# Cosine attention and a Fourier-mixing feed-forward block on one core: new planner costs and step priorities for a list-scheduled kernel

## The chip, the cores and the metric

The kernel runs on one core of a Trainium2 chip. The core has TensorE (matrix multiply, PE in the profile), VectorE (DVE), ScalarE (ACT), GpSimd (POOL) and SyncE (SP), each with its own queue of instructions that it runs in order. Here POOL and SP also issue the DMA transfers. Engines wait for each other through semaphores. The metric is the time on the device, in microseconds (us).

## The reference

```python
q, k, v: (8, 12, 448, 64) float32; w_ch1: (768, 3072); w_ch2: (3072, 768)
q_n = q / (norm(q, axis=-1) + 1e-06);  k_n likewise
attn = softmax(q_n @ k_n.T / tau)                    # per batch and head
x = (attn @ v).transpose(0, 2, 1, 3).reshape(B, S, H * D)      # (8, 448, 768)
mixed = real(fft(fft(x, axis=1), axis=2))
u = x + mixed
un = (u - mean(u)) / sqrt(var(u) + 1e-06)
out = u + relu(un @ w_ch1) @ w_ch2                   # (8, 448, 768) float32
```

## The kernel before

Python code records some 2,900 steps of all 8 batches (`Plan.add`), each with the engines that may run it, an estimated duration, a priority, and what it reads and writes. `Plan.schedule` then places them on a time axis with a list scheduler, and `Plan.emit` writes one queue for each engine in the order that came out, with semaphore waits where a step needs another engine's result. So the order on every engine, and the choice between VectorE, ScalarE and POOL for some steps, follow from the estimated durations (`t_act`, `t_dve` and numbers at each step), the latencies `SEM_LAT` and `PE_LAT`, the modelled DMA flow (`FLOW`), and the priorities, to which the table `SHIFT` adds a number for single steps. Nothing of this runs on the chip; a step that comes later there than the planner thought holds up what stands behind it in its queue.

Step names end in the batch. For each batch b:

- `ld_k`, `ld_q`, `ld_t` load q and k (`t` is the last 64 rows of both). Batches 0 and 1 (`first_norm`) load two groups of six heads; each group g has `ld_k<g>`, `ld_q<g>` and `ld_t<g>` on SP (L661). Batch 1's are written into the place of the second weight matrix (`W2b`) before that is loaded. Later batches (`norm`) load rows into three buffers STG (L788).
- `sq` (ScalarE, L668 and L797) squares, `ss` (VectorE, L670 and L799) sums by head, `ln`, `nrm`, `eps`, `rcp` make the reciprocal norm, `sc` scales (L699 on VectorE or POOL, L806 on POOL). `tk`, `tq`, `tt` transpose on TensorE in batches 0 and 1 (L723, L735, L748); `tr` are DMA transposes into QT and KT from batch 2 on (L812).
- `qk` is a score step on TensorE (L880, L892), `ex` the exponential on ScalarE (L858), `pv` the product with v (L911, L917), `rd` and `x` the division on VectorE.
- `fa`, `f`, `g` fold the rows for the Fourier transform, `fs` (L1004) and `fd` (L1042) are its two matrix products, `u` adds x (L1070, tiles of U), `bs`, `ba`, `ln2`, `rs`, `un` are the layer norm (L1099 to L1108), `tn` (TensorE, L1118, with evictions L1126) or `tru` (DMA, L1129) transposes it into UNT.
- `h` is the first FFN layer (L1176), `relu` its eviction (L1192), `y` and `m` are the second layer (L1207), `fin`, `fa..p` add the residual U on VectorE and POOL (L1239, L1232), `st` and `sc_` store. From batch 1 on the second layer of two tiles at once is done with seven products in place of eight; `s` and `t` are the sums for that.

Attention of batch b + 1 is interleaved with the FFN of batch b on TensorE. `Plan.fill` puts groups of six filler matmuls (`warm`, L1418) into gaps that the planner expects on TensorE. The weights are loaded by POOL in 24 chunks (L592, L593); the first W1 chunk's landing opens batch 1's loads.

The planner's rule for a step that needs results:

```python
else:
    t = max(t, d.end + (SEM_LAT if d.eng != "pe" else PE_LAT) + ...)
...
op.start = t
free[e] = t + d
op.end = t + d
```

Of the kernel before, what the change touches and what calls it, by code (L numbers as in the profile page):

```python
# [24 lines left out]
SEM_LAT = 0.11  # L25
PE_LAT = 0.2
DMA_LAT = 2.0
FLOW = {r"W1_\d+": (3.66, 2.3, 1.25), r"W2_\d+": (3.48, 1.95, 2.6), r"ld_v\d_[01]": (4.35, 1.2, 0.35), r"ld_v\d_\d": (2.92, 1.81, 1.2),
        r"ld_t\d_[01]": (2.95, 1.3, 0.8), r"ld_[kq]\d_[01]": (2.34, 1.92, 0.86), r"ld_t\d_\d": (2.8, 1.75, 1.2), r"ld_[kq]\d_\d": (2.07, 1.65, 0.85),
# [3 lines left out]
    "iota": {0: -840.7}, "cst": {0: -19.8}, "tqd": {0: -145.4}, "tps": {0: -28.6, 1: -75}, "vz0": {0: 9.3}, "vz1": {0: 285.2}, "ldt0": {0:  # L33
# [44 lines left out]
}  # L78

LATE = {r"W[12]_\d+": 1.5, "tmd": 2.0, r"sq\d_2": 4.0, r"sq\d_\d": 2.0, r"ktd\d": 3.0, r"qdup\d": 3.0, r"qk\d._[2-7]": 1.5, r"pv\d\d_[2-7]": 2.0, r"pv\d\d_1": 1.0, r"h\d+_[1-7]": 0.3}
PIECE = {r"sc[KQ]\d_0": 0.95, r"scT\d_0": 0.42, r"sc\d_\d": 0.6, r"f[avm]\dp_\d": 0.54, r"t\d\d": 0.94}
PORT = r"eps\d|f[a01]\d_\d|g\d_\d|u\d+_\d|un\d_\d|s\d\d_\d|t\d\d|sc[KQT]\d_\d"

# [1391 lines left out]
```

## Time and profile before

| | |
|---|---|
| runs | 590.57 us median of 3 (589.21 to 591.01) |
| span of the profiled execution | 590.7 us |
| the profiled execution's own time | the same 590.7 us: the profile has no other |
| busy | PE 571.0, DVE 417.8, ACT 355.0, POOL 211.1 us |
| first FFN matmul (L1176) | 53.67 us |
| last matmul ends | about 587.0 us |
| mean granted clock of TensorE | 0.993 |

Busy time of TensorE counts fillers and work at a lower clock like any other. Where its line in the 40 slices shows a digit under 9, it waited; where it shows 9, the order of its rows says whether the work was real. A wait on another engine matters only where it ends in a wait, a filler or a lower clock of TensorE.

### The profile page before, as it was taken

Reading aid. Unit: us, or ns where it says so; the run is one execution under the profiler, and the core shown is the slowest. Engines: PE = TensorE matmul, PEld = TensorE weight load, DVE = VectorE, ACT = ScalarE, POOL = GpSimd, SP = SyncE. Lnnn points to the kernel's source line nnn. Section 1 sums busy time; section 2 is a strip of 40 time slices with the busy share of each in tenths; the row PEclk is TensorE's granted clock in tenths of the full one; section 3 lists DMA queues with packets and bytes.
Section 4 is the critical chain, followed back from the end, with each engine's and each line's share of the span. In section 5 each row is a group of like instructions: output and inputs, shape, how many; then the busy total and the mean of one; then the engine's idle time right before and its main releaser. Section 6 shows DMA issues by size and latency. Waiting matters only on the chain.

```text
span 590.7 us, 15088 instructions
## 1 busy us (share of the span) xinstructions
PE 571.0 (97%) x6178; PEld 445.1 (75%) x6178; DVE 417.8 (71%) x970; ACT 355.0 (60%) x684; POOL 211.1 (36%) x316
## 2 busy tenths in 40 slices
PE   4897999999999999999999999999999999999997
PEld 3677888687787786878778688778788688778684
DVE  8887878997587767897788678867858547922222
ACT  7994896356874487568746767358566663224140
POOL 7733424346344623703281436440551210200302
PEclk9997999999999999999999999999999999999999
DMA  8999999684396854965496239483294110120101
GB/s 194 184 220 166 162 164 154 152 157 96 106 118 91 144 87 96 171 114 101 50 155 125 52 111 129 108 130 73 54 151 58 28 56 1 62 61 14 47 9 54
DMA packets 187637, 62.12 MB, mean 105 GB/s; under 512 B 166704, under 2 KB 185392, under 8 KB 187568
## 3 DMA queue, kind: packets, MB, share of 16 engines
q1 hardware_dynamic: 129648, 38.35, 33.4%
q0 software_dynamic: 57920, 22.81, 30.7%
q8 instruction: 48, 0.79, 0.6%
q14 instruction: 21, 0.17, 0.1%
HBM read 51.90 MB, written 11.01 MB: 107 GB/s over the span
## 4 chain that ended last, share of the span: by engine, by line
PE 88%; DMA 5%; POOL 2%; issue 1%; SPq 1%; DVE 1%; ACT 0%; POOLq 0%; DVEq 0%
PE PS L1176 37%; PE PS L1207 33%; PE PS L917 5%; PE PS L880 5%; DMA W2b<-in_q_dram 3%; PE PS L1004 2%; PE PS L911 2%; PE PS L1042 2%; DMA W1b<-in_moe_w_ch_dram 1%; SPq L661 1%; DMA KT<-QH 1%; PE PS L892 1%; PE PS L893 1%; POOL VB L838 1%; PE PS L1418 0%
## 5 line engine op out<-in xcount | busy, mean ns | idle before, releaser
L1176 PE MATMUL PS<-UNT,W1b 128*128 128x256 bf16 (+1 forms) x2304 | 237.3, 260 | 0.4 <-DMA UNT<-F 0.4
L1176 PEld LDWEIGHTS PS<-UNT,W1b 128*128 128x128 bf16 x2304 | 199.9, 98 | 23.3 <-issue 3.5
L858 ACT ACTIVATE E<-PS 128x900 bf16<-128x900 f32 (+1 forms) x192 | 148.0, 829 | 28.6 <-PE PS L880 25.0
L1207 PE MATMUL PS<-W2b,HQ 128*128 128x384 bf16 x768 | 133.8, 326 | 0.0
L1192 ACT ACTIVATE HQ<-PS 128x512 bf16<-128x512 f32 x122 | 72.8, 597 | 91.0 <-PE PS L1176 89.6
L806 POOL TENSOR_TENSOR QH<-STG,SM 128x256 bf16<-128x256 f32 x126 | 80.5, 664 | 95.4 <-DVE SM L615 81.9
L1207 PEld LDWEIGHTS PS<-W2b,HQ 128*128 128x128 bf16 x768 | 73.8, 98 | 46.0 <-issue 1.7
L1302 DVE TENSOR_TENSOR HQ<-HQ 128x512 bf16<-128x512 bf16 x141 | 62.6, 463 | 43.8 <-ACT HQ L1192 26.7
L1232 POOL TENSOR_TENSOR OUTB<-OUTB,U 128x192 f32<-128x192 f32 x66 | 39.0, 611 | 140.5 <-ACT OUTB L1227 140.2
L1207 PE MATMUL PS<-TX,HQ 128*128 128x384 bf16 x396 | 70.4, 326 | 0.0
L1207 PEld LDWEIGHTS PS<-TX,HQ 128*128 128x128 bf16 x396 | 37.9, 98 | 23.9 <-issue 0.4
L917 PE MATMUL PS<-VB,E 128*128 128x65 bf16 x1152 | 50.9, 193 | 0.0
L797 ACT ACTIVATE QH<-STG 128x384 f32<-128x384 f32 x84 | 42.3, 519 | 10.2 <-DVE SM L799 8.5
L917 PEld LDWEIGHTS PS<-VB,E 128*128 128x128 bf16 x1152 | 47.5, 97 | 1.1 <-ACT E L858 0.2
L799 DVE TENSOR_REDUCE SM<-QH 128x6 f32<-128x384 f32 x84 | 44.3, 543 | 5.1 <-ACT QH L797 4.6
L1192 DVE TENSOR_SCALAR HQ<-PS 128x512 bf16<-128x512 f32 x40 | 27.6, 691 | 25.9 <-PE PS L1176 25.5
L1261 POOL DMA_INDIRECT out_dram<-OUTB,IDX x20 | 20.6, 1029 | 70.6 <-DVE OUTB L1239 49.4
L911 PE MATMUL PS<-VZ,E 128*128 128x130 bf16 x192 | 41.6, 219 | 0.5 <-DMA VZ<-in_v_dram 0.5
L880 PE MATMUL PS<-QT,KT 64*128 64x225 bf16 x576 | 39.6, 259 | 1.2 <-DMA KT<-QH 0.4
L1070 DVE TENSOR_TENSOR U<-ACG,X 128x384 bf16<-128x384 f32 (+3 forms) x70 | 39.1, 580 | 0.8
L1239 DVE TENSOR_TENSOR OUTB<-PS,OUTB 128x384 f32<-128x384 f32 x33 | 18.2, 553 | 26.6 <-PE PS L1207 24.8
L1227 ACT ACTIVATE OUTB<-PS 128x384 f32<-128x384 f32 x33 | 16.2, 492 | 34.5 <-PE PS L1207 34.3
(133 smaller groups left out, 637.8 us busy)
## 6 DMA issues: line engine op xcount, KB each, us to landing
STG<-in_k_dram SPq DMA_DIRECT2D x18, 384.0 KB, 4.1
STG<-in_q_dram SPq DMA_DIRECT2D x18, 384.0 KB, 3.8
VB<-in_v_dram POOLq DMA_DIRECT2D x24, 192.0 KB, 5.3
W1b<-in_moe_w_ch_dram POOLq DMA_DIRECT2D x12, 384.0 KB, 8.8
W2b<-in_moe_w_ch_dram POOLq DMA_DIRECT2D x12, 384.0 KB, 6.4
out_dram<-OUTB SPq DMA_DIRECT2D x7, 384.0 KB
TX<-in_k_dram SPq DMA_DIRECT2D x2, 576.0 KB, 5.2
TX<-in_q_dram SPq DMA_DIRECT2D x2, 576.0 KB, 6.4
```

Of the source, the lines that this page charges most:

```text
L797: P.add("act", lambda a, sq=sq, src=buf[:, w * x:w * x + w]: a.activation(sq, src, ACTF.Square), t_act(w), pr, f"sq{i}_{b}", reads=bn, wri ...
L799: P.add("dve", lambda v, o=SS[:, i, H // ns * x:H // ns * (x + 1)], sq=sq: v.tensor_reduce(o, sq.rearrange("p (h d) -> p h d", d=DH), AX.X ...
L806: r = v.tensor_tensor(v3(qh)[:, h:h + 4], v3(buf)[:, h:h + 4], RN[:, i, h:h + 4].unsqueeze(2).to_broadcast((128, 4, DH)), AluOp.mult)
L858: return a.activation(o, self.PS[:, bk:bk + nc_, 0:SQ2], ACTF.Exp, scale=1.0 / self.tau)
L880: i = pe.matmul(self.PS[:, bk + h, c0:c0 + NK], self.KT[r, jj, kt * 128:(kt + 1) * 128], self.QT[r, jj, cols], start=True, stop=True)
L911: r = pe.matmul(o, st(6), self.VZ[:, j, :], start=not split, stop=(split and i == 0), skip_group_check=True)
L917: r = pe.matmul(o[:, 65 * h:65 * h + 65], st(2 * kt + h), self.VB[:, kt, 2 * j + h, :], start=(split and i == h == kt == 0), stop=((not sp ...
L1070: return v.tensor_tensor(U[o0:o0 + n, ut, cs].rearrange("p (i e) -> p i e", e=2), src, X[i0:i0 + n, x, cs].rearrange("p (i e) -> p i e", e ...
L1176: r = pe.matmul(self.PS[:, bk, x * n:(x + 1) * n], self.W1b[:, j, ft * 128:(ft + 1) * 128], self.UNT[:, j, cs], start=(j == 0), stop=(j == ...
L1192: return e.activation(o, i, ACTF.Relu) if e is self.nc.scalar else e.tensor_relu(o, i)
L1207: r = pe.matmul(self.PS[:, bk, 0:n], lhs(f), rhs(f), start=(start and f == 0), stop=(stop and f == NF // 2 - 1), skip_group_check=True)
L1302: P.add("dve", lambda v: v.tensor_tensor(cs(o), cs(a), cs(bq), op), 0.46, -0.5, f"{nm}{k}_{b}", reads=rd, writes=hr(o)(k))
```

## The change

1. The two latencies become a pipeline delay for each producer's engine (`PIPE`: the time from the end of an engine's hold to the result) and a hop for each waiting engine (`HOP`). An engine is free after its hold, and the result is there `PIPE` later.
2. The durations are replaced by holds: new formulas, and a table `OCC` by step name.
3. TensorE's step that follows a score step is charged `EXIT`.
4. The planner lets SP issue a load when the fourth DMA before it is nearly done, not the second.
5. `SHIFT` is another table.
6. U's tiles 3 and 6, which hold the last rows of two batches, are written and read under the names of their two halves in every batch, also where a batch uses them as whole tiles. This adds order between batches.

No step is added or taken away, except fillers: 40 groups before, 22 after. Lines of the file move by 14 to 18 (L661 to L679, L668 to L686, L699 to L717, L880 to L898, L1176 to L1194, L1207 to L1225, L1418 to L1435).

```diff
-SEM_LAT = 0.11
-PE_LAT = 0.2
+HOP = {"act": 0.035, "dve": 0.035, "pe": 0.058, "pool": 0.08, "sp": 0.1}
+PIPE = {"act": 0.108, "dve": 0.083, "pe": 0.165, "pool": 0.06, "sp": 0.0}
+EXIT = 0.065
+OCC = {"act": {r"ln\d": 0.195, r"ln2\d_\d": 0.185, ...}, "dve": {...}, "pe": {...}, "pool": {...}}
...
 SHIFT = {
-    "iota": {0: -840.7}, "cst": {0: -19.8}, "tqd": {0: -145.4}, ...
...
+    "ss4_7": {0: -620.6}, "rcp7": {6: -153.2}, "pv00_7": {0: 48.1}, ...
...
-        self.durs = durs
+        self.durs = tuple(next((x for n, x in OCC.get(e, {}).items() if re.fullmatch(n, name)), d) for e, d in zip(engs, durs))
...
-        flow, now, sync = {"sp": [], "pool": []}, 0.0, [None, None]
+        flow, now, sync = {"sp": [], "pool": []}, 0.0, [None] * 4
...
-                    t = max(t, d.end + (SEM_LAT if d.eng != "pe" else PE_LAT) + (...))
+                    t = max(t, d.end + HOP[e] + (...))
...
-                        rt = max(rt, sync[-2].end - DMA_LAT if sync[-2] else 0.0)
+                        rt = max(rt, sync[-4].end - DMA_LAT if sync[-4] else 0.0)
...
+            if e == "pe":
+                if split and op.name[:2] != "qk":
+                    t += EXIT
+                split = op.name[:2] == "qk"
...
-            op.end = t + d
+            op.end = t + d + (PIPE[e] if op.dma is None else 0.0)
...
-    return 0.12 + 0.00089 * n + 0.093 * ptr
+    return 0.061 + 0.000836 * n + 0.093 * ptr
...
-    return 0.1 + n / (960.0 * mode)
+    return 0.067 + n / (960.0 * mode)
...
-                    uadd(A0, 0, 0, 0, 128, hi, 0, f"U{A0}")
+                    uadd(A0, 0, 0, 0, 128, hi, 0, [f"U{A0}z0", f"U{A0}z64"] if A0 in (3, 6) else [f"U{A0}"])
...
-    def unames(self, b, ut):
-        Zt = self.utiles(b)[3]
-        return [f"U{ut}l", f"U{ut}h"] if ut != Zt else [f"U{ut}z{z}{x}" for z in (0, 64) for x in "lh"]
+    def unames(self, ut):
+        return [f"U{ut}l", f"U{ut}h"] if ut not in (3, 6) else [f"U{ut}z{z}{x}" for z in (0, 64) for x in "lh"]
```

More of the change, by code (lines that the diff above doesn't have):

```diff
@@ L190, in schedule @@
         port = []
-        free = {"pe": 1.0, "act": 2.0, "dve": 1.0, "pool": 0.85, "sp": 0.7}
-        flow, now, sync = {"sp": [], "pool": []}, 0.0, [None, None]
+        free = {"pe": 1.0, "act": 2.0, "dve": 1.0, "pool": 0.25, "sp": 0.7}
+        flow, now, sync = {"sp": [], "pool": []}, 0.0, [None] * 4
         def rtime(op, e):
@@ L199, in rtime @@
                 else:
-                    t = max(t, d.end + (SEM_LAT if d.eng != "pe" else PE_LAT) + (op.late if d.dma is not None or d.eng == "pool" and op.late >= 1 else op.margin if e == "pe" else 0.0))
+                    t = max(t, d.end + HOP[e] + (op.late if d.dma is not None or d.eng == "pool" and op.late >= 1 else op.margin if e == "pe" else 0.0))
             return t
@@ L231, in schedule @@
                 put(op)
-        left = len(self.ops)
+        left, split = len(self.ops), False
         slots = {n: [None] * k for n, k in self.pools.items()}
@@ L241, in slot_time @@
                 elif all(u.end is not None for u in t.users):
-                    free_at.append((max(u.end for u in t.users) + SEM_LAT, i))
+                    free_at.append((max(u.end for u in t.users) + 0.04, i))
             n = len(op.acquire)
@@ L340, in fill @@
                     new.deps.add(after)
-                    new.deps.add([o for o in self.order["dve"] if o.end + PE_LAT <= at + 0.1][-1])
+                    new.deps.add([o for o in self.order["dve"] if o.end <= at][-1])
                     new.deps.update(u for a, b, tile in live[bank[0]] if b <= t for u in tile.users[-2:] if u.eng != "pe")
@@ L667, in first_norm @@
                 sq = sqb[g][i]
-                sqo = P.add("act", lambda a, sq=sq, buf=buf: a.activation(sq, buf, ACTF.Square), t_act(64 * n), pg[g], f"sq{nm}{g}_{b}",
+                sqo = P.add("act", lambda a, sq=sq, buf=buf: a.activation(sq, buf, ACTF.Square), t_act(64 * n) + 0.034, pg[g], f"sq{nm}{g}_{b}",
                       reads=names, writes=sqn[g][i], order=[self.exps[-1]] if b else [])
@@ L702, in fn @@
                                                .to_broadcast((128, 3, 2, DH)), AluOp.mult)
-                    sc.append(P.add("dve" if b else ("dve", "pool"), fn, ((t_dve(21 * n), 0.95) if i < 2 else (0.3, 0.42)) if b == 0 else t_dve(21 * n) if i < 2 else 0.3, pg[g] + 0.1 * j, f"sc{nm}{jj}_{b}", reads=names + [f"RN_{g}{i}"],
+                    sc.append(P.add("dve" if b else ("dve", "pool"), fn, ((t_dve(21 * n), 0.95) if i < 2 else (0.2, 0.42)) if b == 0 else t_dve(21 * n) if i < 2 else 0.2, pg[g] + 0.1 * j, f"sc{nm}{jj}_{b}", reads=names + [f"RN_{g}{i}"],
                                     writes=qhn[g][i] if j == 0 else [qhn[g][i][-1] + f"_{j}"],
@@ L797, in norm @@
                 P.add("act", lambda a, sq=sq, src=buf[:, w * x:w * x + w]: a.activation(sq, src, ACTF.Square),
-                      t_act(w), pr, f"sq{i}_{b}", reads=bn, writes=sqn)
+                      t_act(w) + 0.034, pr, f"sq{i}_{b}", reads=bn, writes=sqn)
                 P.add("dve", lambda v, o=SS[:, i, H // ns * x:H // ns * (x + 1)], sq=sq: v.tensor_reduce(
@@ L858, in fn @@
                     return a.activation(o, self.PS[:, bk:bk + nc_, 0:SQ2], ACTF.Exp, scale=1.0 / self.tau)
-                ex = P.add("act", fn, 0.15 + 0.00076 * nc_ * SQ2, pr + 3 + pos, f"ex{ORDER[pos]}_{b}", writes=nm,
+                ex = P.add("act", fn, 0.061 + 0.00083 * nc_ * SQ2, pr + 3 + pos, f"ex{ORDER[pos]}_{b}", writes=nm,
                                      after=[tile.users[0]] + (self.sqb if b == 0 and pos < 2 else []) + (self.fd_ops if pos == 0 else []), tiles=(tile,))
@@ L883, in attn @@
                 rd = [x for ps, kt in st_ for x in qreads(ORDER[ps]) + [f"KT{kt}_{ORDER[ps]}"]]
-                self.last_qk = P.add("pe", fn, 0.195 * len(st_) + 0.2, pj, f"qk{j}{st_[0][1]}_{b}", reads=rd,
+                self.last_qk = P.add("pe", fn, 0.194 * len(st_) + 0.107, pj, f"qk{j}{st_[0][1]}_{b}", reads=rd,
                       tiles=new, acquire=new, margin=0.3, order=([self.last_qk] if self.last_qk else []) + self.pvs[-2:-1])
@@ L954, in fold @@
             P.add("dve", lambda v, i=i, o=o: v.tensor_tensor(AC[:, i:i + 2], X[:, 0:2], X[:, 2:4], o),
-                  t_dve(512, 2) + (0.05 if b else 0.0), pj, f"fa{dj}_{b}", reads=xr, writes=[f"AC{i}"], after=self.snu)
+                  t_dve(512, 2), pj, f"fa{dj}_{b}", reads=xr, writes=[f"AC{i}"], after=self.snu)
         def fdst(eo):
@@ L961, in fold @@
             op = P.add("dve", lambda v, eo=eo, o=o: v.tensor_tensor(fdst(eo), AC[:, :, 0, :], AC[:, :, 1, :], o),
[L962 removed]
+                       t_dve(512, 2), pj, f"f{eo}{dj}_{b}", reads=["AC0", "AC2"],
                        writes=[f"F{eo}{dj}"] + ([f"UN{x}" for x in range(4)] if dj == 0 and eo == 0 else []),
@@ L1071, in fn @@
                                            X[i0:i0 + n, x, cs].rearrange("p (i e) -> p i e", e=2), AluOp.add)
-                self.snu.append(P.add("dve", fn, t_dve(NL) + (0.04 if b else 0.0), pr if b == 0 and ut == A0 else pr + 1 + 0.5 * (ut in (A1, Zt) if b == 1 else b > 0 and kt == 1 and (ut != Yt or o0 > 0)), f"u{kt}_{b}",
+                self.snu.append(P.add("dve", fn, t_dve(NL), pr if b == 0 and ut == A0 else pr + 1 + 0.5 * (ut in (A1, Zt) if b == 1 else b > 0 and kt == 1 and (ut != Yt or o0 > 0)), f"u{kt}_{b}",
                                       reads=[f"X{j}" for j in range(NJ)] + ([f"SN{c}"] if b else []),
-                                      writes=[nm + ("h" if hi else "l")], after=() if b else (fds[c],), tiles=() if b else (tile,)))
+                                      writes=[x + ("h" if hi else "l") for x in nm], after=() if b else (fds[c],), tiles=() if b else (tile,)))
             if kt == 0:
                 for hi in (False, True):
-                    uadd(A0, 0, 0, 0, 128, hi, 0, f"U{A0}")
+                    uadd(A0, 0, 0, 0, 128, hi, 0, [f"U{A0}z0", f"U{A0}z64"] if A0 in (3, 6) else [f"U{A0}"])
                 for hi in (False, True):
-                    uadd(A1, 0, 2, 0, 128, hi, 1, f"U{A1}")
+                    uadd(A1, 0, 2, 0, 128, hi, 1, [f"U{A1}"])
             else:
                 for hi in (False, True):
-                    uadd(Yt, 0, 1, 0, RB, hi, 0, f"U{Yt}")
+                    uadd(Yt, 0, 1, 0, RB, hi, 0, [f"U{Yt}"])
                 P.add("dve", lambda v: v.tensor_copy(U[0:1, A1, :], U[96:97, Yt, :]), t_dve(DM, 4), pr + 1, f"u224_{b}",
@@ L1086, in fft @@
                 for hi in (False, True):
-                    uadd(Yt, 96, 3, 64, 32, hi, 1, f"U{Yt}")
+                    uadd(Yt, 96, 3, 64, 32, hi, 1, [f"U{Yt}"])
                 for hi in (False, True):
-                    uadd(Zt, zo, 3, 0, 64, hi, 1, f"U{Zt}z{zo}")
+                    uadd(Zt, zo, 3, 0, 64, hi, 1, [f"U{Zt}z{zo}"])
         order = self.tiles(b)
@@ L1095, in fft @@
             self.ln_next += 1
-            rn = [f"U{ut}l", f"U{ut}h"] if ut != Zt else [f"U{ut}z{z}{x}" for z in (0, 64) for x in "lh"]
+            rn = self.unames(ut)
             lp = pr if b == 0 and ui == 0 else pr + 1.2 if b and ui < 2 else pr + 2
@@ L1233, in plus @@
                 return r
-            self.P.add("pool", plus, 1.07, -1, f"{nm}p_{b}", reads=[on] + self.unames(b, ut), writes=[on])
+            self.P.add("pool", plus, 1.07, -1, f"{nm}p_{b}", reads=[on] + self.unames(ut), writes=[on])
             return op
@@ L1240, in fin @@
         on = f"OUT{ob}" + "b" * c
-        return self.P.add("dve", fn, t_dve(384), -1, f"{nm}_{b}", reads=[on] if src == "out" else self.unames(b, ut), writes=[on],
+        return self.P.add("dve", fn, t_dve(384), -1, f"{nm}_{b}", reads=[on] if src == "out" else self.unames(ut), writes=[on],
                           after=(op,), tiles=(tile,))
@@ L1301, in comb @@
             rd = sorted(set(hr(a)(k) + hr(bq)(k)))
-            P.add("dve", lambda v: v.tensor_tensor(cs(o), cs(a), cs(bq), op), 0.46, -0.5, f"{nm}{k}_{b}", reads=rd, writes=hr(o)(k))
+            P.add("dve", lambda v: v.tensor_tensor(cs(o), cs(a), cs(bq), op), 0.335, -0.5, f"{nm}{k}_{b}", reads=rd, writes=hr(o)(k))
         for i in range(0, len(tiles), 2):
@@ L1366, in fn @@
                     return r
-                P.add("dve", fn, 0.94, 190, f"{nm}{k}", reads=rd, writes=wr + old * (nm != "t3"), after=af)
+                P.add("dve", fn, 0.867, 190, f"{nm}{k}", reads=rd, writes=wr + old * (nm != "t3"), after=af)
     def copy(self, o, i, n, mode, prio, name, **kw):
```

11 lines of the change are left out of this document (8 added, 3 removed), and 95 rows, old and new, of the table SHIFT.

## The prediction

> **What bounds the kernel now.** First the page: the busy time of each engine says which one to follow.
>
> ```profile
> span 590.7 us, 15088 instructions
> PE 571.0 (97%) x6178; PEld 445.1 (75%) x6178; DVE 417.8 (71%) x970; ACT 355.0 (60%) x684; POOL 211.1 (36%) x316
> ```
>
> TensorE is busy for 97% of the span, so a change of order can win only what is not real work on it: idle time, the filler matmuls of L1418 that the planner puts into gaps, and time at a lower clock. The groups by line give the fillers' price:
>
> ```profile
> L1418 PE MATMUL PS<-TX 128*128 128x128 bf16 x174 | 14.9, 244 | 8.6 <-DVE UNT L533 7.2 <-DVE SM L615 0.5 <-DVE SM L670 0.4
> L1418 PE MATMUL PS<-W1b 128*128 128x128 bf16 x66 | 4.5, 219 | 0.2 <-DVE SM L799 0.2
> ```
>
> That is 19.4 us of filler beside 20 us of idle time (590.7 - 571.0). The first group lies before the feed-forward part (FFN) starts and costs only what the waits there cost. The other 66 matmuls stand later, each in front of work that is due. So I asked for the waits around the start of the FFN, from 43 to 54 us, and the chain there:
>
> ```profile
> ACT W2b L668 <- DMA W2b<-in_q_dram: 2.8, 1, 2.8
> PE PS L1118 <- DVE F L1108: 2.6, 1, 2.6
> ```
> ```profile
> 31.26 17.75 DMA W2b<-in_q_dram
> 49.03 1.16 ACT W2b L668
> ...
> 50.72 0.68 DVE F L1108
> ```
>
> A load of batch 1's q, the last of eight transfers in SP's queue, lands 17.75 us after its issue. ScalarE's next instruction, the square of that load (L668), stands waiting for it, and behind it in the same queue stand the two small steps (L1103, L1105) of batch 0's layer norm. VectorE's normalise (L1108) waits for those, TensorE's transposes (L1118) for that, and the first FFN matmul for these. ScalarE's and TensorE's timelines there:
>
> ```profile
> 49.03 1.16 ACT L668 ACTIVATE W2b<-W2b 128x1152 f32<-128x1152 f32 x1 [2.84 <-DMA W2b<-in_q_dram]
> ```
> ```profile
> 48.00 0.81 PE L723 MATMUL PS<-TX,QH 128*128 128x128 bf16 x6 [0.22 <-DVE QH L699]
> 53.67 0.42 PE L1176 MATMUL PS<-UNT,W1b 128*128 128x128 bf16 x2
> ```
>
> The table by stretches, cut where the granted clock changes, shows the second half of the price:
>
> ```profile
> 50.13:56.96 6.83, 5.51 (x52) 5.51 (x53) 5.18 (x11) 2.96 (x9) 2.49 (x4) 0.50 1.30 166
> ```
>
> While TensorE waited, its clock fell to 0.50 and stayed there for 6.83 us, 3.3 us of them after the FFN had begun at 53.67. After 57 us TensorE is busy without a break but for one place, the end of batch 1's FFN. Its timeline:
>
> ```profile
> 179.86 3.44 PE L1176 MATMUL PS<-UNT,W1b 128*128 128x256 bf16 x30
> 183.14 4.06 PE L1207 MATMUL PS<-W2b,HQ 128*128 128x384 bf16 x24
> 187.04 4.06 PE L1207 MATMUL PS<-TX,HQ 128*128 128x384 bf16 x24
> ...
> 194.84 0.50 PE L1418 MATMUL PS<-W1b 128*128 128x128 bf16 x6
> 195.17 2.11 PE L1207 MATMUL PS<-TX,HQ 128*128 128x384 bf16 x12
> 197.12 1.87 PE L1418 MATMUL PS<-W1b 128*128 128x128 bf16 x30
> 198.92 0.56 PE L880 MATMUL PS<-QT,KT 64*128 64x225 bf16 x8
> 199.73 0.84 PE L1418 MATMUL PS<-W1b 128*128 128x128 bf16 x12 [0.24 <-DVE SM L799]
> 200.99 7.38 PE L1176 MATMUL PS<-UNT,W1b 128*128 128x256 bf16 x66 [0.42 <-DMA UNT<-F]
> 208.75 0.56 PE L880 MATMUL PS<-QT,KT 64*128 64x225 bf16 x8 [0.38 <-DMA KT<-QH]
> ```
>
> From 197.12 to 200.99 only one score step is real work. Starts give the rates: (183.14 - 179.86)/30 = 0.109 us for a matmul of the first FFN layer, (187.04 - 183.14)/24 = 0.163 for one of the second.
>
> **The change part by part.** The sum is made against the profiled execution's 590.7; the median of the runs is 590.57, so nothing is added between them. The constants (a hold and a pipeline delay instead of one latency) issue nothing; they act through the order alone.
>
> *Start of the FFN.* Batch 1's q and k loads are written in another order. The names are the sides k and q; the 64-row ones are the tails.
>
> The loads of batch 1 in SP's queue, before:
>
> ```order
> L661 DMA W2b<-in_k_dram 128x6x192
> L661 DMA W2b<-in_q_dram 128x6x192
> L661 DMA W2b<-in_q_dram 64x6x64
> L661 DMA W2b<-in_k_dram 64x6x64
> L661 DMA W2b<-in_q_dram 64x6x64
> L661 DMA W2b<-in_k_dram 64x6x64
> L661 DMA W2b<-in_k_dram 128x6x192
> L661 DMA W2b<-in_q_dram 128x6x192
> ```
>
> And of the change:
>
> ```order
> L679 DMA W2b<-in_k_dram 128x6x192
> L679 DMA W2b<-in_q_dram 128x6x192
> L679 DMA W2b<-in_q_dram 64x6x64
> L679 DMA W2b<-in_k_dram 64x6x64
> L679 DMA W2b<-in_k_dram 128x6x192
> L679 DMA W2b<-in_q_dram 128x6x192
> L679 DMA W2b<-in_q_dram 64x6x64
> L679 DMA W2b<-in_k_dram 64x6x64
> ```
>
> The rows hide which head group a load belongs to. In the code's names the q load for which ScalarE waits (ld_q0_1) was the last row of the first list and is the second of the new one; last is now a small tail (ld_t1_1), which ScalarE squares only after the first score step of batch 1. So 2.84 us of ScalarE's wait go. L1103 is then held by VectorE's statistics (L1101), and L1108 by the two scale steps (L699) ahead of it:
>
> ```profile
> 47.27 0.17 DVE L1101 BATCH_NORM_AGGREGATE MV<-ACG 128x2 f32<-128x12 f32 x1
> 47.39 1.03 DVE L699 TENSOR_TENSOR QH<-W2b,SM 128x384 bf16<-128x384 f32 x2
> 51.78 0.55 DVE L1070 TENSOR_TENSOR U<-PS,X 97x384 bf16<-97x384 f32 x1
> 60.09 0.56 DVE L1126 CAST UNT<-PS 128x384 bf16<-128x384 f32 x1
> ```
>
> The statistics are there at 47.44, the two small ScalarE steps after them take about half a us, and the scales end at 48.42: L1108 starts there and not at 50.72. One of the two evictions that follow (L1126) moves from ScalarE to VectorE, where it comes after another scale (about 0.5) and an addition (0.55): 48.42 + 0.68 + 0.5 + 0.55 + 0.56 = 50.7. I put the first FFN matmul at 50.8 against 53.67: **2.9 us won**. If the clock stays at 1.00, the 3.3 us that the FFN ran at half speed shrink by half: **1.6 us won**. Ahead of this the change moves three scales from VectorE to POOL, in front of the first weight load, which opens batch 1's loads; and it takes a negation (L578) from POOL:
>
> ```profile
> 8.17 2.48 POOL L578 TENSOR_SCALAR HQ<-CS 128x900 bf16<-128x900 bf16 x1
> 20.82 1.07 POOL L699 TENSOR_TENSOR QH<-TX,SM 128x384 bf16<-128x384 f32 x1 [0.98 <-DVE QH L699]
> ```
>
> Three times 1.07 against 2.48: I take 0, with 1 us either way. Batch 0's exponentials on ScalarE are as many as before: 0, also with 1 us either way.
>
> *Fillers.* There were 11 groups of six after the FFN's start and are none. Two single places:
>
> ```profile
> 64.34 0.49 PE L1418 MATMUL PS<-W1b 128*128 128x128 bf16 x6
> 122.15 0.83 PE L1418 MATMUL PS<-W1b 128*128 128x128 bf16 x12
> ```
>
> What a filler holds is its row less about 0.16 of pipeline: 0.33 and 0.67, **1.0 us won** if the work behind them is ready. At the second, batch 1's layer norm must be transposed in time; it is ordered ahead of more of VectorE's queue than before, so I count it.
>
> *End of batch 1's FFN.* TensorE's rows there, before (L880 is the first score step of batch 3, QT and KT its transposed inputs, L1176 the first FFN layer of batch 2):
>
> ```order
> L1207 MATMUL PS<-W2b,HQ 128x384 x24
> L1207 MATMUL PS<-TX,HQ 128x384 x24
> L1207 MATMUL PS<-W2b,HQ 128x384 x24
> L1418 MATMUL PS<-W1b 128x128 x6
> L1207 MATMUL PS<-TX,HQ 128x384 x12
> L1418 MATMUL PS<-W1b 128x128 x30
> L880 MATMUL PS<-QT,KT 128x225 x8
> L1418 MATMUL PS<-W1b 128x128 x12
> L1176 MATMUL PS<-UNT,W1b 128x256 x66
> L880 MATMUL PS<-QT,KT 128x225 x8
> ```
>
> And now:
>
> ```order
> L1194 MATMUL PS<-UNT,W1b 128x256 x36
> L1225 MATMUL PS<-W2b,HQ 128x384 x24
> L1225 MATMUL PS<-TX,HQ 128x384 x4
> L898 MATMUL PS<-QT,KT 128x225 x8
> L1225 MATMUL PS<-TX,HQ 128x384 x20
> L1225 MATMUL PS<-W2b,HQ 128x384 x16
> L898 MATMUL PS<-QT,KT 128x225 x8
> L910 MATMUL PS<-QT,KTD 128x225
> L911 MATMUL PS<-QT,KTD 128x225
> L1225 MATMUL PS<-W2b,HQ 128x384 x8
> L1225 MATMUL PS<-TX,HQ 128x384 x4
> ```
>
> Batch 3's attention starts inside batch 1's FFN, and no filler is left. Batch 2's first layer comes 36 x 0.109 + 84 x 0.163 + about 3 for the attention steps between = 20.6 us after its last transform, against 21.1 before (200.99 - 179.86), but with work where filler stood, and its second normalise stands ahead of VectorE's wait for an output tile, not behind it. Won: 0.33 (195.17 - 194.84), 1.80 (198.92 - 197.12), 0.24, 1.26 (200.99 - 199.73), and the 0.38 at 208.75: **4.0 us**. Were the transposed input no earlier than before, 0.5 of it would be a wait.
>
> *Names of residual rows.* Tiles 3 and 6 of U now carry the same names in every batch, so writes of one batch wait for the adds of an earlier one. Those adds belong to an FFN that ends well ahead of the write: 0. Were that cover gone, VectorE would stand for one POOL addition:
>
> ```profile
> L1232 POOL TENSOR_TENSOR OUTB<-OUTB,U 128x192 f32<-128x192 f32 x66 | 39.0, 611 | 140.5 <-ACT OUTB L1227 140.2
> ```
>
> two halves of 0.61, 1.2 us, with TensorE's next eviction on VectorE behind it.
>
> *What comes due instead.* The filler at 64.34 stood right behind the first of batch 1's transposes of q (0.4 us), which so began 10.3 us after the first FFN matmul, or 8.7 at full clock. The new order has four groups of six fewer ahead of them:
>
> ```profile
> 60.94 3.18 PE L1176 MATMUL PS<-UNT,W1b 128*128 128x128 bf16 x54
> ```
>
> 24 x 0.056 = 1.3 us. The scales on VectorE that they need win nothing by that: between 0 and 1.3, I take **1.0 us lost**. The rest of the order is denser, with score steps pulled forward in nearly every batch; for waits that I don't see I take **1.3 us**, a little over what three rows above add up to (0.24 + 0.42 + 0.38); bounds 0 and 5.
>
> Sum: 590.7 - 2.9 - 1.6 - 1.0 - 4.0 + 1.0 + 1.3 = 583.5.
>
> **The rivals.**
>
> *The lead is eaten by the weights (587.0).* The last two chunks of the first layer's weights are issued by POOL as earlier ones land:
>
> ```profile
> 52.40 0.82 POOL L592 DMA_DIRECT2D W1b<-in_moe_w_ch_dram  x1 [1.16 <-DMA W1b<-in_moe_w_ch_dram]
> ```
> ```profile
> W1b<-in_moe_w_ch_dram POOLq DMA_DIRECT2D x12, 384.0 KB, 8.8
> ```
>
> With the median landing the last is there at 61.2; before, its readers, the last 24 of the 54 matmuls from 60.94, began at 62.6; now they would at 60. That is 1.2 us, and if the earlier start meets the same queues again at batch 1's values and at the second layer's weights, 3.5 of the 4.5 us are gone. For it: the total of bytes is unchanged. Against it: no matmul waits for a weight now.
>
> *The clock falls all the same (586.3).* It fell at 50.13, in a wait that began at 48.8 and lasted 2.64 us. There are fewer fillers before the FFN now (132 matmuls against 174), and the short waits between batch 1's transposes remain. A full stretch on solid work costs 5.51/2 = 2.8 us more than forecast. Against it: from 20 to 30 us the clock stayed at 1.00 with TensorE busy for 8.79 of 10 us:
>
> ```profile
> 20.00:30.00 10.00, 8.79 (x155) 6.53 (x155) 8.37 (x22) 8.58 (x13) 6.22 (x7) 1.00 1.28 228
> ```
>
> [...]
>
> *Fillers for waits (590.2).* The gaps were there because inputs come late; without filler TensorE waits as long, and an earlier start is met by a later wait, and of the 7.2 us some 0.5 stay. Against it: in both large gaps the late input was held by an order, not by its work.
>
> *Score steps too early (slower: 597.4).* Now 36 x 0.109 + 64 x 0.163 + about 0.7 = 15.0 us lie between batch 2's last transform (end 179.86) and the score step that needs the last k of batch 3; it had its input at
>
> ```profile
> 183.86 0.52 ACT L797 ACTIVATE QH<-STG 128x384 f32<-128x384 f32 x1
> 195.90 0.55 DVE L799 TENSOR_REDUCE SM<-QH 128x6 f32<-128x384 f32 x1
> 201.18 2.07 POOL L806 TENSOR_TENSOR QH<-STG,SM 128x256 bf16<-128x256 f32 x3 [0.18 <-issue]
> 203.27 5.44 DMA KT<-QH
> ```
>
> 208.7, 28.9 us after. TensorE runs in order, with the whole FFN behind that step. If this chain came no earlier, 13.9 us would be lost: 597.4. Slower than before begins where it comes less than 6.7 us earlier (13.9 - 7.2). Against it: the square stood at 183.86, and its reduction waited 12 us in VectorE's queue; the change sets both squares, the reductions and the scale ahead of batch 2's transforms or close behind. For it: a transpose landing of 5.44 us leaves little, and batches 5 and 6 are pulled forward alike.
>
> **How the numbers follow.** Forecast 0.60; weights 0.13; clock 0.09; fillers for waits 0.05; too early 0.13. The time is the forecast's, 583.5. Its own range is 579.5 (the two 1 us terms and the unseen waits all for it) to 587. The whole range, 579.5 to 589.5, takes in the weights and the clock and leaves out some 0.19. A measurement of this kernel tells about 0.3%, 1.8 us, from no change: faster 0.60 + 0.13 + 0.09 = 0.82, same 0.05, slower 0.13.
>
> **What would show it.** Right: no wait of L686 for a load, the first L1194 near 51 us, one stretch of clock 1.00 from 13 us on, no idle time over 0.5 us near 190, and the FFN's end 7 us earlier. Wrong: L898 waiting for a KT or QT transpose in several batches; a wait of L1194 for W1b; the clock at 0.50 after 45 us; or first matmuls of batch 1's or 2's FFN waiting for UNT as long as the fillers lasted.

## The result and the profile after

| | median | executions | ratio to the kernel before |
|---|---|---|---|
| forecast | 583.5 us (579.5 to 589.5) | | |
| before | 589.27 us (587.36 to 591.65) | 20 | |
| changed | 589.04 us (586.96 to 593.79) | 20 | 0.9998, 95% interval 0.9977 to 1.0018 |
| changed, two later measurements | 587.54 and 587.96 us | 12 and 12 | 0.9955 (0.9933 to 0.9976) and 0.9978 (0.9951 to 1.0005) |

Each ratio is to the executions of before in the same measurement. In the first there is no difference; over all three the changed kernel is 0 to 0.45% faster. The 1.2% of the forecast did not come. The profiled execution of the changed kernel:

```profile
span 586.4 us, 14876 instructions
PE 566.3 (97%) x6070; PEld 437.5 (75%) x6070; DVE 416.9 (71%) x971; ACT 353.7 (60%) x681; POOL 215.1 (37%) x318
```

Its own time is 588.35 us: about 2.0 us lie around the span. Of before only a span was known: the 590.7 us that the table above also calls a time is one, and before's later executions show 1.8 us around theirs. So the forecast, worked out from a span, was a span too, and with 2.0 us around it 585.5 as a time.

The start of the FFN, in TensorE's timeline and the table by stretches (PEclk is the third number from the end):

```profile
51.31 0.49 PE L1435 MATMUL PS<-TX 128*128 128x128 bf16 x6 [0.21 <-DVE U L1088]
51.73 5.52 PE L1194 MATMUL PS<-UNT,W1b 128*128 128x128 bf16 x96
```
```profile
50.00:57.00 7.00, 6.74 (x113) 6.22 (x113) 6.81 (x16) 4.13 (x11) 3.18 (x4) 1.00 1.27 176
```

The FFN begins at 51.73, 1.9 us earlier than in the profile of before, at full clock. The stretch of 57 to 180 us, first before, then changed, shows the other side:

```profile
57.00:180.00 123.00, 123.00 (x1390) 96.88 (x1389) 97.63 (x225) 86.10 (x174) 52.43 (x72) 1.00 0.92 137
```
```profile
57.00:180.00 123.00, 120.36 (x1320) 93.25 (x1318) 99.29 (x230) 86.09 (x172) 54.44 (x75) 1.00 0.97 141
```

TensorE never idled there and now idles for 2.6 us. Its list of waits from 54 to 580 us names them (us in total, times, longest):

```profile
PE PS L1060 <- ACT E L1033: 1.5, 1, 1.5
PE PS L753 <- ACT TX L1210: 0.5, 1, 0.5
PE PS L1136 <- DVE F L1126: 0.4, 1, 0.4
PE PS L1194 <- DMA UNT<-F: 0.3, 1, 0.3
PE PS L1022 <- DVE ACG L1001: 0.2, 1, 0.2
PE PS L766 <- ACT QT L732: 0.2, 1, 0.2
PE PS L1225 <- DVE OUTB L1256: 0.2, 1, 0.2
```

Together 3.3 us; the same list of before has 1.4. The longest stands before batch 2's second Fourier product; the chain of waits there:

```profile
167.17 5.68 DMA QT<-QH
172.85 2.44 issue
175.29 0.52 ACT QH L815
175.81 0.82 ACT E L1033
176.63 0.05 issue
176.68 1.36 PE PS L1060 x14
```

ScalarE's square (L815) writes into a buffer QH that a transpose of batch 3 still reads. The transpose was issued at 167.17 and took 8.1 us to land, and the square starts at 175.29. The load that the square reads was issued at 166.59 and landed 4.1 us later, so it was not what held the square. Behind the square in ScalarE's queue stands the eviction (L1033) for which TensorE waits. The DMA issues from 159 to 177 us (count, median us from issue to landing), first changed, then before:

```profile
QT<-QH SPq DMA_TRANSPOSE x4, 8.0
KT<-QH SPq DMA_TRANSPOSE x2, 8.3
```
```profile
QT<-QH SPq DMA_TRANSPOSE x2, 4.1
...
KT<-QH SPq DMA_TRANSPOSE x1
```

The change puts six transposes of batch 3 where three were, and the median one into QT takes twice as long.

### The profile page after: what moved, and what is told of

Its sections match the earlier page's. It is cut to its first block, busy times and chain, and to the rows that moved or that the text cites. A ratio compares the mean times of both kernels' runs of the same rounds, so it can differ in the third digit from the quotient of the medians.

```text
span 586.4 us, 14876 instructions
## 1 busy us (share of the span) xinstructions
PE 566.3 (97%) x6070; PEld 437.5 (75%) x6070; DVE 416.9 (71%) x971; ACT 353.7 (60%) x681; POOL 215.1 (37%) x318
## 4 chain that ended last, share of the span: by engine, by line
PE 83%; DVE 9%; DMA 3%; issue 2%; ACT 1%; POOL 1%; SPq 0%; POOLq 0%; DVEq 0%; ACTq 0%
PE PS L1194 35%; PE PS L1225 31%; PE PS L935 5%; PE PS L898 5%; PE PS L1060 2%; PE PS L929 2%; PE PS L1022 2%; DVE U L1088 1%; DMA TX<-in_q_dram 1%; DMA QT<-QH 1%; PE PS L910 1%; DVE QH L717 1%; DVE HQ L1319 1%; ACT E L876 1%; PE PS L911 1%
## 5 line engine op out<-in xcount | busy, mean ns | idle before, releaser
L1194 PE MATMUL PS<-UNT,W1b 128*128 128x256 bf16 (+1 forms) x2304 | 234.2, 259 | 0.4 <-DMA UNT<-F 0.3
L1194 PEld LDWEIGHTS PS<-UNT,W1b 128*128 128x128 bf16 x2304 | 198.8, 98 | 23.0 <-issue 2.6
L1210 ACT ACTIVATE HQ<-PS 128x512 bf16<-128x512 f32 x129 | 77.0, 597 | 97.8 <-PE PS L1194 96.9
L1225 PE MATMUL PS<-W2b,HQ 128*128 128x384 bf16 x768 | 133.9, 326 | 0.0
L824 POOL TENSOR_TENSOR QH<-STG,SM 128x256 bf16<-128x256 f32 x126 | 84.0, 694 | 97.8 <-DVE SM L633 72.4
L1225 PEld LDWEIGHTS PS<-W2b,HQ 128*128 128x128 bf16 x768 | 73.5, 98 | 46.4 <-issue 2.2
L1249 POOL TENSOR_TENSOR OUTB<-OUTB,U 128x192 f32<-128x192 f32 x66 | 39.8, 624 | 139.5 <-ACT OUTB L1244 138.7
L1225 PE MATMUL PS<-TX,HQ 128*128 128x384 bf16 x396 | 70.9, 326 | 0.2 <-DVE OUTB L1256 0.2
L1225 PEld LDWEIGHTS PS<-TX,HQ 128*128 128x128 bf16 x396 | 37.8, 98 | 24.2 <-issue 0.7
L815 ACT ACTIVATE QH<-STG 128x384 f32<-128x384 f32 x84 | 42.5, 519 | 14.6 <-DVE SM L817 9.9
L898 PE MATMUL PS<-QT,KT 64*128 64x225 bf16 x576 | 40.0, 261 | 1.2 <-ACT E L876 0.7
L1210 DVE TENSOR_SCALAR HQ<-PS 128x512 bf16<-128x512 f32 x33 | 22.7, 687 | 17.9 <-PE PS L1194 17.9
L898 PEld LDWEIGHTS PS<-QT,KT 64*128 64x128 bf16 x576 | 22.7, 94 | 15.8 <-issue 5.4
```

The costliest lines, as they stand in the source:

```text
L815: P.add("act", lambda a, sq=sq, src=buf[:, w * x:w * x + w]: a.activation(sq, src, ACTF.Square), t_act(w) + 0.034, pr, f"sq{i}_{b}", reads ...
L824: r = v.tensor_tensor(v3(qh)[:, h:h + 4], v3(buf)[:, h:h + 4], RN[:, i, h:h + 4].unsqueeze(2).to_broadcast((128, 4, DH)), AluOp.mult)
L898: i = pe.matmul(self.PS[:, bk + h, c0:c0 + NK], self.KT[r, jj, kt * 128:(kt + 1) * 128], self.QT[r, jj, cols], start=True, stop=True)
L1194: r = pe.matmul(self.PS[:, bk, x * n:(x + 1) * n], self.W1b[:, j, ft * 128:(ft + 1) * 128], self.UNT[:, j, cs], start=(j == 0), stop=(j == ...
L1210: return e.activation(o, i, ACTF.Relu) if e is self.nc.scalar else e.tensor_relu(o, i)
L1225: r = pe.matmul(self.PS[:, bk, 0:n], lhs(f), rhs(f), start=(start and f == 0), stop=(stop and f == NF // 2 - 1), skip_group_check=True)
```

## The experiments

Theory 1: the one profiled execution of before was not typical of it. Theory 2: the gain is real and is lost again in new waits. Both turned out to hold a part.

**Both kernels once more.** 

> The kernel before, unchanged, profiled and timed again. Theory 1 (the one profiled execution of before was longer than its usual runs: span 590.7 us, where 20 later runs of the kernel had a median time of 589.27, which is about 587.3 us of span if 2 us lie around the span as in the changed kernel's profile, 588.35 against 586.4): a second profile has a span near 587, with no stretch of clock 0.50 at the start of the FFN or a shorter wait of ScalarE for the q load, and first FFN matmul at 51 to 52.5 us. Theory 2 (the late load and the half clock belong to this kernel, and the changed kernel loses its gain elsewhere): first FFN matmul at 53.7 and 5 to 7 us of half clock again, spans near 590.

> The changed kernel, unchanged, profiled and timed again. Theory 1: nothing but the usual spread; median 589, spans 585 to 592, and the profile has first FFN matmul near 51.7 and the wait of TensorE near 174.9 (1.5 us) again. Theory 2: the same median, since the waits between 57 and 293 us (1.5 at 57 to 62, 1.6 at 174.9, 1.3 in three places later, together 4.4 us) are part of its order and are there in every execution. Where the two profiles of this kernel differ shows what its runs vary by: if it is the start (before 52 us) by over 1 us, transfers decide it; if it is the granted clock, a short stretch of 0.50 shows.

Before: 591.68 us, ratio 1.0009 (0.9988 to 1.0029) to its own other runs. Its second profile has a span of 591.0, ScalarE's wait of 2.74 us again, and the clock:

```profile
49.80 1.16 ACT L668 ACTIVATE W2b<-W2b 128x1152 f32<-128x1152 f32 x1 [2.74 <-DMA W2b<-in_q_dram]
```
```profile
54.24 1.93 PE L1176 MATMUL PS<-UNT,W1b 128*128 128x128 bf16 x28
```
```profile
47.84:51.25 3.41, 1.14 (x12) 0.62 (x12) 1.12 (x4) 1.42 (x3) 0.77 (x2) 1.00 1.23 155
51.25:54.66 3.41, 2.63 (x25) 2.64 (x26) 3.07 (x6) 2.15 (x6) 1.07 (x2) 0.50 1.02 130
```

So theory 1 fails as it was put: the wait belongs to the kernel. But the clock does not fall each time, nor does the FFN begin as late each time. The third profile in this order up to the FFN is that of before without its late fillers (below): the wait is there, the clock stays at 1.00, and the FFN begins at 51.97. ScalarE's row in it:

```profile
47.99 1.16 ACT L668 ACTIVATE W2b<-W2b 128x1152 f32<-128x1152 f32 x1 [2.51 <-DMA W2b<-in_q_dram]
```

That is only 0.2 us behind the changed kernel. Of 102 executions of before in the three later jobs, 46 had a mean granted clock of 0.999 or more, with a median time of 589.2 us; the other 56 had 591.7. The profile that the forecast stood on (0.993) is of the second kind.

Changed: 587.54, span 585.6 in the second profile, FFN from 51.57. The wait for L1033 is not there, since the transpose landed earlier (issued at 166.79; the square starts 6.8 us later and not 8.1), but the one before batch 3's FFN is longer. Rows of SP, ScalarE and TensorE:

```profile
166.79 3.48 SPq L830 DMA_TRANSPOSE QT<-QH  x2
```
```profile
173.60 0.52 ACT L815 ACTIVATE QH<-STG 128x384 f32<-128x384 f32 x1 [0.72 <-issue]
```
```profile
260.11 2.14 PE L1194 MATMUL PS<-UNT,W1b 128*128 128x256 bf16 x18 [1.14 <-DMA UNT<-F]
```

**One step of before moved.** In this and most of the following kernels the plan is made as it was, and then a step is put elsewhere in its engine's queue; `ahead(queue, step, other)` puts it in front of another.

```diff
+ act = self.P.order["act"]
+ sq = act.pop(... "sqQ0_1")
+ act.insert(... "relu0_0", sq)
```

> The kernel before, with one step moved: the square of batch 1's q load (L668, the one that waited 2.84 us) stands on ScalarE behind batch 0's first layer norm steps and transposes' evictions, just ahead of the first relu. Everything else is the order of before. Theory 1: the wait is short in most runs, so 0 to 1.5 us are won: ratio 0.997 to 1.000. Theory 2: the first FFN matmul comes at 51 and the clock stays at 1.00: 2.9 + 1.6 = 4.5 us won, ratio 0.992. In both, the square's own 1.15 us now stands ahead of the first relu, which costs TensorE nothing as long as its PSUM has free banks.

588.05 us, ratio 0.9961 (0.9943 to 0.9979), and a clock of 0.999 or 1.00 in all 12 executions, 587.12 to 589.37. In ScalarE's and TensorE's timelines the square waits for nothing, and the FFN begins at 50.12:

```profile
50.33 1.18 ACT L668 ACTIVATE W2b<-W2b 128x1152 f32<-128x1152 f32 x1
```
```profile
50.12 3.86 PE L1176 MATMUL PS<-UNT,W1b 128*128 128x128 bf16 x66
```

This one move, against 590.43 for before in that job, wins 2.4 us; the whole change won 2.9 in the same job. The forecast's mechanism at the start is shown, and that taking the wait away secures the clock: before kept it in 19 of its 35 executions of that job, this kernel in all 12. The forecast's 4.5 us are not won: against before's executions with a lower clock (591.8 us in that job) it is 3.8, against the others (589.1) 1.0.

**The late fillers of before left out**, alone and with the square moved.

```diff
- self.P.fill(first, self.est - 20.0, self.id_op, warm(self.W1b[:, 0, 0:128]), 0.75)
```

> The kernel before without the 66 filler matmuls that stand behind the start of the FFN (the second call of the fill is left out); the order is otherwise the same. The prediction's term: each filler group holds up ready work by its length, 1.0 us at 64.34 and 122.15 and part of 4.0 us near 195; if all of the 4.5 us of the group were in the way of ready work, ratio 0.992. Rival (fillers for waits): the work behind them is not ready, TensorE waits instead, 0 to 0.5 us won, ratio 0.999 to 1.000. Slower than before, if the waits without filler lower the clock: a stretch of 0.50 after 197 us, up to 2.8 us lost, ratio up to 1.005.

> The kernel before with the square of batch 1's q load moved (as in the run with the later square, 588.05 us at a ratio of 0.9961, clock 1.00 in all its executions) and without the 66 fillers behind the start of the FFN (alone, without the move: 592.56, ratio 1.0031). Theory A (the clock falls only at the start of the FFN, in the wait for the square; the late fillers do nothing for it): clock 1.00 again, ratio 0.994 to 0.997, since fillers in front of waits cost nothing and those of 64 and 122 us are worth at most 1.0. Theory B (without the fillers near 195 us the waits there, 1.5 and 2.0 us in the profile without fillers, lower the clock): clock 0.997 or less in most executions, 1.7 us or more lost for each stretch of 3.4 us at 0.50, ratio 0.999 or more.

Alone: 592.56, ratio 1.0031 (1.0006 to 1.0056), slower by 0.3%, and 11 of 12 executions have a clock of 0.990 to 0.997. Its profiled execution, the fastest and the only one at 1.00, has waits in the fillers' place:

```profile
194.97 0.56 PE L880 MATMUL PS<-QT,KT 64*128 64x225 bf16 x8 [1.30 <-DMA QT<-QH]
197.42 7.37 PE L1176 MATMUL PS<-UNT,W1b 128*128 128x256 bf16 x66 [1.88 <-DVE SM L615]
```

With the square moved: 590.49, ratio 0.9992 (0.9972 to 1.0013), so the 2.4 us of the move are nearly gone, and 11 of 12 executions have a clock of 0.993 to 0.997. The profile of the second shows where, in TensorE's timeline and the stretches:

```profile
194.15 0.57 PE L880 MATMUL PS<-QT,KT 64*128 64x225 bf16 x8 [1.29 <-DMA QT<-QH]
196.97 2.39 PE L1176 MATMUL PS<-UNT,W1b 128*128 128x256 bf16 x13 [2.26 <-DVE U L1070]
```
```profile
194.16:197.57 3.41, 1.15 (x14) 0.86 (x15) 3.38 (x10) 2.93 (x7) 1.99 (x3) 1.00 1.01 249
197.57:200.99 3.42, 3.42 (x18) 2.38 (x17) 0.47 (x3) 1.00 (x3) 1.28 (x3) 0.50 1.14 252
```

Without fillers TensorE waits 1.29 and 2.26 us in their place, and the clock is at 0.50 for the next 3.42 us of solid work, 1.7 us lost: the 66 matmuls of the first layer that begin at 196.97 take 9.03 us, against 7.37 in the run above. So the fillers near 195 us held up nothing, and they kept the clock. (Both runs leave out all 66; what those at 64 and 122 us did alone, no run shows.) In the order of before, the rival "fillers for waits" is right.

**The input near 195 us brought forward in before**, with the square moved.

```diff
+ ahead("dve", "un1_2", "fin31_1")      # second normalise before two output additions
+ ahead("sp", "tru1_2", "tr5_3")        # its transpose before one of K or Q
+ del pe[i - 2:i]                       # two filler groups before h0_2
+ ahead("pe", "h17_2", "qk02_3"); ahead("pe", "h6_2", "qk02_3"); ahead("pe", "h7_2", "qk02_3")
```

> The kernel before with the square moved as in the run with the later square, and around 195 us: batch 2's second normalise (L1108) stands ahead of two output additions (L1239) on VectorE, its transpose ahead of one of K on SP, the two last filler groups ahead of batch 2's first FFN step are left out, and the score step that waited 0.52 us for K stands three FFN steps later. The prediction's reading (the late input there is held by an order, not by its work): batch 2's FFN begins 1.3 to 1.8 us earlier, ratio to the kernel with the later square 0.997, so about 586.7 us. Rival (fillers for waits): the transposes share SP's queue and the DMA engines, the input comes as late as before, or the score step later: 0 to 0.5 us won, about 588.

589.37, ratio 0.9992 (0.9966 to 1.0019): nothing won against before, and the 2.4 us of the square, measured in another job, are lost again. In its profile batch 2's FFN does begin sooner after batch 1's (196.6 - 119.7 = 76.9 us, against 195.9 - 118.0 = 77.9 with the square moved alone), but the next score step waits 1.53 us, and a weight was waited for in batch 0's FFN:

```profile
208.39 0.56 PE L880 MATMUL PS<-QT,KT 64*128 64x225 bf16 x8 [1.53 <-ACT E L858]
```
```profile
58.85 1.50 PE L1176 MATMUL PS<-UNT,W1b 128*128 128x128 bf16 x24 [1.03 <-DMA W1b<-in_moe_w_ch_dram]
```

The order did hold the input, as the forecast read it, but the time came back as a wait for the exponential 12 us later. Whether the 1.0 us for the weight come from the earlier FFN (the first rival) or from this execution, one profile does not tell; with the square moved alone the FFN began as early and no such wait stands.

**The changed kernel with its new waits taken away.** First the eviction alone, beside the unchanged kernel:

```diff
+ ahead("act", "te0_2", "sq6_3")        # eviction L1033 before the square L815
```

> The changed kernel, unchanged, a third time, beside which the others of this job are read. Two measurements gave a ratio to the kernel before of 0.9998 and of 0.9955. If both kernels only spread by what their loads and their clock do in an execution, this one lies between, 0.995 to 1.000, and its profile has either the wait at 174.9 us (1.5) or the longer one before batch 3's FFN (1.1 against 0.35), or a stretch at 0.50 clock, whose place shows where the fillers are missing.

> The changed kernel with one step moved: on ScalarE the eviction (L1033) that batch 2's second Fourier product waits for stands ahead of the square (L815) of a load of batch 3, not behind it. Theory A (the load's landing, 8.7 us after its issue in one profile of the changed kernel and 7.3 in the other, decides how long that square waits, and TensorE with it: 1.5 us idle in the one, 0 in the other): TensorE's wait of L1060 for L1033 is gone in the profile, and the time is 0 to 1.5 us under the changed kernel's of this job, with fewer long executions. Theory B (the spread of the changed kernel comes from the granted clock, which falls in some executions since no fillers are left): no change of the spread, the long executions are still those with a clock under 0.998.

What the two texts call a load's landing is, by the chain shown above, the landing of a transpose that frees the square's buffer. Unchanged: 587.96 us, 586.88 to 591.91, in its profile a wait of 0.2 us at the place. Eviction first: 587.31, ratio 0.9953 (0.993 to 0.9976), 586.7 to 588.43: the long executions are gone, though 7 of the 12 still have a clock of 0.993 to 0.997. So theory A. The 7 have a median of 587.33 us, the other 5 of 587.26. Its profile (clock 0.993) shows why such a clock sets it back by nothing: the clock is at 0.50 from 13.97 for 6.8 us, and there the changed kernel's first profile is as slow without a record of it (0.94 us for its first score step, where before's takes 0.56; the rows stand below). The mean takes the time ahead of a profile's first record of the clock for 1.00, and in the other profiles of the changed order that record stands at 19.1 to 20.0 us.

```profile
10.55:13.97 3.42, 1.77 (x20) 1.11 (x21) 3.04 (x10) 3.19 (x7) 2.85 (x5) 1.00 2.89 180
13.97:17.38 3.41, 3.02 (x24) 2.18 (x24) 2.96 (x5) 2.33 (x5) 2.71 (x4) 0.50 2.86 94
```

Then batch 3's second normalise as well:

```diff
+ ahead("act", "te0_2", "sq6_3")
+ ahead("dve", "un1_3", "bs3_3")        # second normalise L1126 before two statistics L1117
```

> The changed kernel with the eviction first, and also batch 3's second normalise (L1126) ahead of two statistics steps (L1117) on VectorE, so that its transpose is issued about 1 us earlier. Theory A: the waits of TensorE for L1033 near 175 us and for UNT near 260 us (0.35 to 1.1 us) are gone: 0.4 to 2.6 us under the changed kernel of this job, ratio to it 0.996 to 0.999. Theory B: the median moves by the 0.4 to 1.1 us of the second wait alone and the upper end of the executions stays.

586.09 us, ratio 0.9936 (0.9913 to 0.996), 585.68 to 587.28. Its profile has a span of 583.8, and TensorE's waits in the FFN are down to 1.2 us:

```profile
PE PS L753 <- ACT TX L1210: 0.3, 1, 0.3
PE PS L766 <- ACT QT L732: 0.3, 1, 0.3
PE PS L1225 <- DVE OUTB L1256: 0.2, 1, 0.2
PE PS L1136 <- DVE F L1126: 0.2, 1, 0.2
PE PS L898 <- DVE U L1088: 0.2, 1, 0.2
```

This version beats both kernels: by 3.6 us before and by 1.9 us the changed one, medians of the same job.

**The constants alone.** 

> The changed kernel with the table SHIFT of before: the new holds, delays, the four loads ahead and the residual rows' names alone. Theory A (the constants act through the order alone, and the numbers of a table fit only the costs they were made for): another order with more waits of TensorE, slower than before by 2 to 10 us, ratio 1.003 to 1.017. Theory B (the constants are the better description and carry the gain by themselves): as fast as the changed kernel, ratio 0.995 to 0.999.

596.31 (7 executions), ratio 1.0095 (1.0063 to 1.0126), slower. The largest group of TensorE's waits in its profile, after that at the kernel's start (in this file L1218 is the second FFN layer, L1249 an output addition on VectorE):

```profile
PE PS L1218 <- DVE OUTB L1249: 3.5, 4, 1.6
```

The new durations alone do not carry the gain: this table of priorities does not fit them. Of the parts of the change, the four loads ahead move nothing at all: planned with two ahead, the same queues come out, step for step. Of the order that the residual rows' names add, the changed kernel's profile shows one wait on VectorE, and none on TensorE that follows from it:

```profile
430.00 1.02 DVE L1088 TENSOR_TENSOR U<-ACG,X 64x384 bf16<-64x384 f32 x2 [1.39 <-POOL OUTB L1249]
```

## Why the prediction was wrong

Three steps of it failed; the rest held.

1. **The sum's base.** "The sum is made against the profiled execution's 590.7; the median of the runs is 590.57, so nothing is added" set a span equal to a time (1.8 us) and took one execution, in which the clock fell and the load came late, for the kernel. Before's median of 589.27 us is a span of about 587.5, so 3.2 of the 7.2 us were forecast against an execution that much longer than the usual one. Of the rest of the miss, 2.9 us lie between the forecast span and the profiled one (steps 2 and 3), 0.7 between that execution and the changed kernel's median, and 0.2 in what lies around the spans. Over the later jobs before's executions with the clock held have 589.2 us, the others 591.7; against them the changed kernel's 588.0, the median of all its 44, is a gain of 1.2 and of 3.7 (before's median differs by up to 1.4 between the jobs). So in about every second execution of before much of what was to be won was there already.

2. **The unseen waits.** Taken at 1.3 us, with 1.0 for batch 1's q transposes. The waits are 3.3 us in one profile and, by the same list, 2.8 in the other. The bounds of 0 to 5 hold them. The q transposes' part fits in size (L753 and L766, together 0.7), but by the profile they waited for ScalarE's evictions (L1210, L732) and not for VectorE's scales. Two waits were not foreseen, L1033 before the Fourier product and UNT before batch 3's FFN, and taking them away won 1.9 us.

3. **The lead.** 2.9 forecast; 53.67 - 51.73 = 1.9. ScalarE's wait for the load went as foreseen, but "the statistics are there at 47.44" was a time of the old order. In the new one batch 0's attention itself ends later: VectorE's additions of its Fourier product, which the statistics follow, start 1.4 us later. Before, then changed:

```profile
43.77 2.42 DVE L1070 TENSOR_TENSOR U<-PS,X 128x384 bf16<-128x384 f32 x5 [0.16 <-PE PS L1042]
```
```profile
45.19 1.95 DVE L1088 TENSOR_TENSOR U<-PS,X 128x384 bf16<-128x384 f32 x4
...
48.69 0.16 DVE L1119 BATCH_NORM_AGGREGATE MV<-ACG 128x2 f32<-128x12 f32 x1
```

The term that failed is "I take 0, with 1 us either way" for what stands ahead of batch 0's attention; the second 0, for its exponentials, held. They begin 1.1 us later and end 1.2 later. The first score step and the first exponential, before and then changed:

```profile
15.93 0.56 PE L880 MATMUL PS<-QT,KT 64*128 64x225 bf16 x8
16.34 0.92 ACT L858 ACTIVATE E<-PS 128x900 bf16<-128x900 f32 x1
```
```profile
16.85 0.94 PE L898 MATMUL PS<-QT,KT 64*128 64x225 bf16 x8
17.45 0.92 ACT L876 ACTIVATE E<-PS 128x900 bf16<-128x900 f32 x1
```

The same eight matmuls take 0.94 us and not 0.56: in the changed order TensorE is still slower there. A step of four score matmuls takes 0.55 us at 18.69 and 0.37 at 19.81. Its first record of the clock, at 1.00, stands at 19.1 us, before's at 12.6; ahead of it the table by stretches prints 1.00 without a record. So the sign "one stretch of clock 1.00 from 13 us on" did not hold. In the six profiles with before's order at the start, that record stands at 10.8 to 17.1 us; in four of five with the changed order at 19.1 to 20.0, and in the fifth the clock is at 0.50 from 13.97 to 20.8. How much of the 1.2 us that makes, and how much the inputs, no run singles out: in the second profile of before the clock came up at 17.1 us, the first exponential began at 16.9, and the last ended as early as in the first profile.

With the old order and the square moved, the FFN begins at 50.12, so the wait's own 2.9 were not too much against the first profile.

In spans: forecast 583.5, profiles 586.4, 585.6 and 585.8. Of the 2.9 us missed in the first, 1.0 are the lead; from the FFN's start to the end of the span 4.3 were forecast, and (590.7 - 53.67) - (586.4 - 51.73) = 2.4 came. Of those 1.9 missed, about 0.6 are the waits (3.3, against 2.3 forecast and 0.4 of before's that the sum left in); 1.3 lie in small places that no run singles out.

One bound of the prediction does not come out of its terms: 583.5 less the two 1 us terms and the unseen waits is 580.2, not 579.5. Nothing above rests on it.

What held: no wait for the q load, clock 1.00 through the FFN's start, no filler after it. The gap of batch 1's FFN closed (no wait of TensorE from 178 to 205 us), and by the change of order, not by leaving out fillers: left out alone, they leave waits and a lower clock.

Of the rivals, "fillers for waits" has the mechanism right for the order of before. "Score steps too early" has the direction right: batch 3's preparation pulled forward does collide, though in ScalarE's queue and for 1.5 us, not in a score step for 13.9. "The clock falls all the same" did not show at the start of the FFN in any profile of the changed order. "The lead is eaten by the weights" did not show either: no matmul of the changed kernel waits for a weight after 54 us in any of its three profiles. That rival's sum had its readers at 60 us, which leaves out the 1.6 us of clock; with them it is 58.1.

## What to carry to other kernels

Before a sum is made against a profile, ask whether that execution is the kernel's usual one: compare its granted clock and its time, not its span, with those of other executions. In a queue that runs in order, look for the step that waits for a transfer and has another engine's input behind it: moving that one step won 2.4 us in one order and cut the long executions of the other. The fillers in front of late work were free here and held the clock, so take a filler for a sign of a wait until a run without it shows otherwise.

## What the runs showed of the hardware

The clock fell also where TensorE had worked in the 3.41 us before: it was busy for 1.14 (before, second profile), 1.15 (square moved, no fillers), 1.75 (before, first profile) and 1.77 us (eviction first) of them, and the half clock lasted 3.41 or 6.83 us. In three profiles the changes lie on a grid. With the square moved and no fillers the first record of the clock is at 13.26 us and the fall at 197.57, 54.0 steps of 3.413 us later. In the first profile of before they are at 12.58, 50.13, 56.96 and 589.43 us, with 11.0, 2.0 and 156.0 such steps between them, and in that of the changed kernel at 19.11 and 585.72, 166.0 steps apart. In two profiles the place of the waits on this grid fits whether the clock fell. With the square moved and no fillers the wait of 2.26 us lay whole within one step, busy for 1.15 us. In the profile of before without late fillers, at a mean clock of 1.00, the waits of 1.30 and 1.88 us were divided between two steps, busy for 1.81 and 1.83 us. But no limit of busy time comes out of these runs: with the constants alone, the clock fell after a step busy for 2.01 us.

A transpose into QT took 8.0 us from issue to landing (median of four) in the stretch of 159 to 177 us, where the changed kernel moves 144 GB/s, against 4.1 (of two) in before, which moves 106 there. In two executions of the changed kernel the one that holds the square differed by 1.3 us (8.1 and 6.8 from its issue to the square's start).
